# VectorE's order in a fused retention and feed-forward kernel: the product with h ahead of the product of d and r

## The chip, the cores and the metric

The kernel runs on one core of a Trainium2 chip. The metric is the device time of one execution in microseconds (us). Times of the trace are counted from the span's start; a single instruction's duration is given in us or ns.

## What is computed

Three layers follow one another: a retention (an attention with a decay in place of a softmax), a feed-forward layer whose activation is h times tanh(softplus(h)), and a layer of eight experts to which tokens are assigned greedily by their logits. The change lies in the feed-forward layer.

```python
def _moe_ref(x, w_in, w_out):
    h = x @ w_in                       # 2304 x 512 times 512 x 2048
    sp = np.where(h > 20.0, h, np.log1p(np.exp(np.minimum(h, 20.0))))
    g = h * np.tanh(sp)
    return (g @ w_out)
# around it: x = retention(q, k, v); out[mask_e] = relu(x[mask_e] @ w1[e]) @ w2[e]
```

## The kernel before

The first part of the kernel interleaves the retention, the conversion of the feed-forward weights and the feed-forward itself. The 2304 tokens are nine blocks of 256, the 2048 hidden units sixteen slices of 128; `plan()` lists the 144 steps (block n, slice f). One loop runs over the steps i, and every engine works through its instructions in the order in which this loop issues them (the order is written out by hand).

A step has these pieces, with what each engine does in them:

- `ff_h` (L317): twelve TensorE matmuls make h for 128 hidden units and 256 tokens in PSUM (`ph`). Weights and activations are split into a high and a low part, so there are three products for each of four slices of the inner dimension. Two steps share a PSUM bank, and there are two such banks; a bank is written again when both its steps have been read.
- `ff_a1`: ScalarE's tanh, square and scaling (L326 to L328) make two tables d for positive and negative halves; VectorE multiplies them (L334).
- `ff_a2` (L339): VectorE's reciprocal of that product, in place. The result is r.
- `ff_b1` (L344, or L346 and L347): u is the product of d, its halves swapped, and r. As long as weights are being converted (`alone`) this is one instruction of 128x256 on VectorE, and r is a buffer of its own; later it is two instructions of 128x128 on GpSimd. In the last step it is two on VectorE.
- `ff_b2` (L352): VectorE's product of (u - 1) with h, read from PSUM. It is issued for step i-1 in step i. Only then is `ph` of that step free.
- `ff_b3` (L358, L359): ScalarE rounds the result to its high part gh, and VectorE (during conversion) or GpSimd subtracts it to get the low part gl. It is issued for step i-2 in step i.
- `ff_y` (L411, in the last block L447): six (or twelve) TensorE matmuls add to the output, three steps later.

The conversion of one weight slice takes a step too: a load of 512 KB into one of two `raw` buffers, on SP's queue (L140); `x1` and `c` on ScalarE (L159, L156); `x` and `a` on VectorE (L163, L168, both reading two operands from SBUF); `h` on ScalarE (L174), the rounding to a high part; and `l` on GpSimd (L177), the subtraction that leaves the low part. `a` is the last reader of its raw buffer, and the next load is issued behind it. In the order of the loop, `x` and `a` of the current slice come first, then the step's own pieces with `x1` of the next slice between `ff_a1` and `ff_b3`, then `h` and `c`.

In a step with conversion VectorE's order is thus L163, L168, L334, L359, L339, L344, L352, and ScalarE's is L326, L327, L328, L159, L358, L174, L156. In the steps up to about 84 us pieces of the retention come in between (GpSimd's share of them is L228 and L233), and some steps behind that have no conversion.

Of the kernel before, what the change touches and what calls it, by code (L numbers as in the profile page):

```python
# [64 lines left out]
def plan():  # L65


    spread = lambda a, b, n: [a + (b - a) * k // (n - 1) for k in range(n)]
    own = {i: (0, f) for f, i in enumerate([0, 1, 2, 3] + spread(6, ENDS[0], NF - 4))}
    free = [i for i in range(3 * NF) if i not in own]  # L70
    lead = [i for i in free if i < BEGIN2]
    rest = [i for i in free if BEGIN2 <= i]
    near = [i for i in rest if i <= ENDS[1]]
    ones = lead + [near[k] for k in spread(1, len(near) - 1, NF - len(lead))]
    own.update({i: (1, f) for f, i in enumerate(ones)})
    own.update({i: (2, f) for f, i in enumerate(i for i in free if i not in ones)})
    steps = [own[i] for i in range(3 * NF)]
    steps += [(n, f) for n in range(3, NB) for f in range(NF)]
    return steps


def first_part(ctx, tc, att, att_ht, att_hn, dtab, qtab, ktab, stab, wi, wo, wgb, ydram, L, constants, cst, begin, grid):
    nc = tc.nc
# [15 lines left out]
    steps = plan()  # L99
# [42 lines left out]
    class convert:  # L142
# [18 lines left out]
        def x(self):  # L161
            w0 = self.w0
            nc.vector.scalar_tensor_tensor(w0, self.w1, 0x80000000, w0, op0=ALU.bitwise_and,  # L163
                                           op1=ALU.bitwise_or)
# [144 lines left out]
    def ff_h(n, f, i):  # L309
        xh, xl = x_block(n)  # L310
        if i % 2 == 0:
            hbank[0] = psum.tile([P, 2, TB], F32, tag=("ph0", "ph1")[i // 2 % 2], name="ph")
        ph = hbank[0][:, i % 2, :]
        k = 0
        for kt in range(KT):
            for w, x in ((winh, xh), (winl, xh), (winh, xl)):
                nc.tensor.matmul(ph, w[f][:, kt, :], x[:, kt, :], start=(k == 0), stop=(k == 11))  # L317
                k += 1
        q2[n, f] = ph

    def ff_a1(n, f, i, alone):

        ph = q2[n, f]
        d = work.tile([P, 2, P], F32, tag="d", name="d", bufs=2)
        df = d.rearrange("p a b -> p (a b)")
        nc.scalar.activation(df, ph, AF.Tanh, scale=0.5)  # L326
        nc.scalar.activation(df, df, AF.Square, bias=half_b, scale=-0.5)  # L327
        nc.scalar.activation(df, df, AF.Copy, bias=0.5, scale=0.5)  # L328
        u = work.tile([P, 2, P], F32, tag="u", name="u", bufs=3)
        r = u[:, 0, :]  # L330
        if alone:

            r = work.tile([P, DM], BF, tag="scr", name="r").bitcast(F32)[:, :P]
        nc.vector.tensor_mul(r, d[:, 0, :], d[:, 1, :])  # L334
        inv[n, f] = (d, u, r, alone)

    def ff_a2(n, f):
        r = inv[n, f][2]
        nc.vector.reciprocal(r, r)  # L339

    def ff_b1(n, f, eng):
        d, u, r, alone = inv.pop((n, f))
        if alone:
            eng.tensor_mul(u, d[:, ::-1, :], r[:, None, :].to_broadcast([P, 2, P]))  # L344
        else:
            eng.tensor_mul(u[:, 1, :], d[:, 0, :], r)  # L346
            eng.tensor_mul(u[:, 0, :], d[:, 1, :], r)  # L347
        gt[n, f] = u.rearrange("p a b -> p (a b)")

    def ff_b2(n, f):  # L350
        g = gt[n, f]
        nc.vector.scalar_tensor_tensor(g, g, -1.0, q2.pop((n, f)), op0=ALU.add, op1=ALU.mult)  # L352

    def ff_b3(n, f, eng):
        g = gt[n, f]
        gh = work.tile([P, TB], F32R, tag="gh", name="gh", bufs=3)
        gl = work.tile([P, TB], F32R, tag="gl", name="gl", bufs=3)
        nc.scalar.activation(gh, g, AF.Copy)  # L358
        eng.tensor_sub(gl, g, gh.bitcast(F32))  # L359
        gt[n, f] = (gh, gl)  # L360
# [170 lines left out]
    for i in range(len(steps) + YL):  # L531
        new = i < len(steps)
        if i == 20:
            constants()
        if i == 62:
            stage.__exit__(None, None, None)
            late = tc.tile_pool(name="late", bufs=1)
            WG = late.__enter__().tile([P, E, DM], F32, name="WG")
            nc.sync.dma_start(WG, wgb)
        if now:  # L540
            now.x()
            now.a()
        if old:
            old.l()
        if new:
            n, f = steps[i]
            ff_h(n, f, i)
            for x in slots.get(i, []):
                x()
            ff_a1(n, f, i, bool(now or old))  # L550
        if nxt and i in CONV:
            nxt.x1()
        if new:

            eng = nc.vector if now or old else nc.gpsimd
            if i > 1:
                ff_b3(*steps[i - 2], eng)
            ff_a2(n, f)
            ff_b1(n, f, nc.vector if i == len(steps) - 1 else eng)
            if i:  # L560
                ff_b2(*steps[i - 1])
        if i == len(steps) - 1:
            ff_b2(n, f)
            ff_b3(*steps[i - 1], nc.gpsimd)
            ff_b3(n, f, nc.vector)
        if now:
            now.h()
        old, now = now, None
        if nxt and i in CONV:
            now, nxt = nxt, convert() if done[0] < len(parts) else None  # L570
            now.c()
        for k in range(2 if i % 4 == 0 or TAIL <= i < POP2 else 1):
            if idle:
                idle.pop(0)()
        if late and i > TAIL + BEGIN and not idle:
            late = late.__exit__(None, None, None)
            soon.extend(begin())
        if i >= YL:
            ff_y(*steps[i - YL], i)
# [840 lines left out]
def build(tc, ap, out):  # L1420
    nc = tc.nc
    with ExitStack() as ctx:
        pp = ctx.enter_context(tc.tile_pool(name="pp", bufs=1))
        dp = ctx.enter_context(tc.tile_pool(name="dp", bufs=1, space=bass.MemoryType.DRAM))
        cp = ctx.enter_context(tc.tile_pool(name="cp", bufs=1))
        ctx.enter_context(tc.manual_schedule())
        L = pp.tile([P, NT, E], F32, name="L")
        ydram = dp.tile([N, DM], F32, name="ydram")
        cst = {}
        start = []  # L1430
        cs = ExitStack()

        def begin():
            start.append(Search(cs, tc, L, cst))
            return start[0].early()

        with ExitStack() as c1:
            first_part(c1, tc, ap["att"], ap["att_ht"], ap["att_hn"], ap["dtab"], ap["qtab"],
                       ap["ktab"], ap["stab"], ap["wi"], ap["wo"], ap["wgb"], ydram, L, lambda: constants(cp, tc, ap, cst), cst, begin, lambda *a: Grid(cs, tc, L, cst).pieces(*a))
        keep = ctx.enter_context(tc.tile_pool(name="keep", bufs=1, reuse_waits="tile"))  # L1440
        L0 = keep.tile([P, NT, E], F32, name="L0")
        nc.gpsimd.tensor_copy(L0, L)
        with ExitStack() as c2:
            flag = second_part(c2, tc, L, ydram, ap["wx"], cst, out, start[0], True, L0)
            again = nc.values_load(flag[0:1, 0:1], min_val=0, max_val=1)
        cs.close()
        with tc.If(again != 0):
            with ExitStack() as c3:
                general_constants(c3, tc, ap, cst)
                second_part(c3, tc, L0, ydram, ap["wx"], cst, out, Start(c3, tc, L0, cst), False)  # L1450
# [15 lines left out]
def constants(cp, tc, ap, cst):  # L1466
    nc = tc.nc
    load_constants(cp, tc, ap, cst, (("ident", [P, P], F32), ("J", [P, NJ + 1], F32), ("SCL", [P, 3], F32),
                                     ("pri", [P, E], F32), ("tri", [P, P], BF), ("io", [P, 96], BF),
                                     ("pcv", [P, NT, 2], BF), ("WGN", [P, KT, E], F32)))  # L1470
    cst["ones"] = cp.tile([P, P], BF, name="c_ones")
    nc.vector.memset(cst["ones"], 1.0)
# [69 lines left out]
```

## Time and profile before

| | us |
|---|---|
| median of 3 runs | 856.23 |
| lowest and highest of them | 855.38, 856.98 |
| the profiled execution | 856.09 |
| its span, first to last instruction | 854.2 |

| engine | busy us | share of the span |
|---|---|---|
| TensorE matmuls | 781.2 | 91% |
| VectorE | 556.4 | 65% |
| GpSimd | 476.0 | 56% |
| ScalarE | 438.5 | 51% |

The shares are averages over unlike stages. The steps with weight conversion run from 31 to 171 us of the span, the other feed-forward steps up to about 551 us, the expert layer from there to the end. A line of the timeline has an instruction's start, its duration, engine, source line and operands; in square brackets stands how long its engine had stood idle before it, and what ended that. An instruction's recorded end can lie a little behind the start of the next one on the same engine.

### The profile page before, as it was taken

How to read it: one execution, taken by the hardware profiler on the slowest of the kernel's cores; microseconds unless marked ns; L12 is line 12 of the kernel's file. 1: busy time of each engine (PE TensorE's matmuls, PEld its weight loads, DVE VectorE, ACT ScalarE, POOL GpSimd, SP SyncE). 2: the span in 40 equal slices, each digit the busy share in tenths (PEclk: the TensorE clock that was granted, in tenths of full speed). 3: DMA queues.
4: the chain of work that ended last, by engine and by line, in shares of the span. 5: the costliest groups of instructions: out<-in, count | busy, mean ns of one | idle time of the engine just before them, and what ended most of it. 6: DMA issues, size and time to landing. Idle time of an engine off the chain costs nothing.

```text
span 854.2 us, 16245 instructions
## 1 busy us (share of the span) xinstructions
PE 781.2 (91%) x6151; PEld 711.9 (83%) x6151; DVE 556.4 (65%) x1271; ACT 438.5 (51%) x963; POOL 476.0 (56%) x541
## 2 busy tenths in 40 slices
PE   6787778799999999999999999939999999999993
PEld 5676566698899888889888989838999899999993
DVE  4797999964654689788897885576566643532210
ACT  2676777754554445454455464423344543654521
POOL 2533332354554666667666664413777986977911
PEclk9798999999999999999999999957999999999997
DMA  8535332201024120111210000033665656555411
GB/s 310 179 117 181 140 130 101 74 26 48 30 73 148 52 74 25 51 52 49 76 50 26 1 26 2 2 133 127 200 184 175 186 174 185 163 159 185 127 30 31
DMA packets 27320, 87.63 MB, mean 103 GB/s; under 512 B 4448, under 2 KB 5600, under 8 KB 27104
## 3 DMA queue, kind: packets, MB, share of 16 engines
q1 hardware_dynamic: 24160, 77.06, 27.8%
q0 software_dynamic: 3072, 9.44, 3.4%
q8 instruction: 50, 0.82, 0.4%
q14 instruction: 38, 0.31, 0.1%
HBM read 77.05 MB, written 9.44 MB: 101 GB/s over the span
## 4 chain that ended last, share of the span: by engine, by line
PE 70%; DVE 12%; issue 6%; ACT 4%; DMA 4%; POOL 2%; SPq 0%; DVEq 0%; POOLq 0%; ACTq 0%
PE ph L317 20%; PE hp L1257 9%; PE op L1271 8%; PE b_E L411 8%; PE b_F L411 7%; PE cnt L972 2%; DVE r L339 2%; DMA raw<-in_wi_dram 2%; DVE u L344 1%; PE b_A L219 1%; DVE raw L163 1%; PE b_D L248 1%; DVE hot L868 1%; PE b_E L447 1%; PE b_F L447 1%
## 5 line engine op out<-in xcount | busy, mean ns | idle before, releaser
L317 PE MATMUL ph<-xh,winh 128*128 128x256 f32 x576 | 165.6, 287 | 16.8 <-DVE u L352 9.7
L317 PE MATMUL ph<-xl,winh 128*128 128x256 f32 x576 | 163.1, 283 | 0.2 <-DVE xl L255 0.2
L317 PE MATMUL ph<-xh,winl 128*128 128x256 f32 x576 | 163.2, 283 | 0.0
L811 POOL TENSOR_TENSOR wxl<-wraw,wxh 128x1024 fp32r<-128x1024 f32 x60 | 142.4, 2397 | 31.3 <-ACT wxh L809 30.8
L359 POOL TENSOR_TENSOR gl<-u,gh 128x256 fp32r<-128x256 f32 x114 | 86.0, 754 | 90.1 <-ACT gh L358 89.4
L317 PEld LDWEIGHTS ph<-xh,winh 128*128 128x128 f32 x576 | 110.5, 192 | 29.0 <-DVE u L352 15.1
L326 ACT ACTIVATE d<-ph 128x256 f32<-128x256 f32 x144 | 54.9, 381 | 135.7 <-PE ph L317 122.0
L317 PEld LDWEIGHTS ph<-xh,winl 128*128 128x128 f32 x576 | 111.3, 193 | 4.5
L317 PEld LDWEIGHTS ph<-xl,winh 128*128 128x128 f32 x576 | 111.5, 194 | 0.4 <-DVE xl L255 0.4
L339 DVE RECIPROCAL u<-u 128x128 f32<-128x128 f32 x113 | 107.7, 953 | 3.9
L334 DVE TENSOR_TENSOR u<-d 128x128 f32<-128x128 f32 x113 | 45.4, 402 | 63.6 <-ACT d L328 55.8
L346 POOL TENSOR_TENSOR u<-d,u 128x128 f32<-128x128 f32 x112 | 52.5, 469 | 52.5 <-DVE u L339 52.3
L809 ACT ACTIVATE wxh<-wraw 128x1024 fp32r<-128x1024 f32 x64 | 67.3, 1052 | 17.9 <-DMA wraw<-in_wx_dram 17.9
L327 ACT ACTIVATE d<-d,half_b 128x256 f32<-128x256 f32 x144 | 73.5, 510 | 4.7
L347 POOL TENSOR_TENSOR u<-d,u 128x128 f32<-128x128 f32 x112 | 68.4, 610 | 8.8
L328 ACT ACTIVATE d<-d 128x256 f32<-128x256 f32 x144 | 60.2, 418 | 4.6
L358 ACT ACTIVATE gh<-u 128x256 fp32r<-128x256 f32 x144 | 58.0, 403 | 4.1 <-DVE u L352 4.1
L368 DVE SCALAR_TENSOR_TENSOR scr<-y,WG 128x512 bf16<-128x512 f32 x64 | 55.3, 864 | 0.4
L1248 DVE SCALAR_TENSOR_TENSOR htl<-hp,hth 128x288 fp32r<-128x288 f32 x64 | 28.4, 454 | 40.4 <-ACT hth L1260 38.8
L352 DVE SCALAR_TENSOR_TENSOR u<-u,ph 128x256 f32<-128x256 f32 x144 | 53.9, 375 | 0.2
L1260 ACT ACTIVATE hth<-hp 128x288 fp32r<-128x288 f32 x64 | 26.2, 409 | 52.9 <-PE hp L1257 46.7
L177 POOL TENSOR_TENSOR wol<-y,woh 128x512 fp32r<-128x512 f32 x16 | 20.7, 1292 | 54.5 <-ACT woh L174 54.5
(271 smaller groups left out, 1942.3 us busy)
## 6 DMA issues: line engine op xcount, KB each, us to landing
wraw<-in_wx_dram SPq DMA_DIRECT2D x64, 512.0 KB, 4.5
att<-in_att_dram SPq DMA_DIRECT2D x32, 512.0 KB, 5.2
raw<-in_wi_dram SPq DMA_DIRECT2D x16, 512.0 KB, 3.5
raw<-in_wo_dram SPq DMA_DIRECT2D x16, 512.0 KB, 3.3
ydram<-y SPq DMA_DIRECT2D x9, 512.0 KB, 2.8
WG<-in_wgb_dram SPq DMA_DIRECT2D x1, 2048.0 KB, 7.7
att<-in_att_ht_dram SPq DMA_DIRECT2D x4, 256.0 KB, 4.1
att<-in_att_hn_dram SPq DMA_DIRECT2D x4, 256.0 KB, 4.7
```

The costliest lines, as they stand in the source:

```text
L317: nc.tensor.matmul(ph, w[f][:, kt, :], x[:, kt, :], start=(k == 0), stop=(k == 11))
L327: nc.scalar.activation(df, df, AF.Square, bias=half_b, scale=-0.5)
L328: nc.scalar.activation(df, df, AF.Copy, bias=0.5, scale=0.5)
L339: nc.vector.reciprocal(r, r)
L347: eng.tensor_mul(u[:, 0, :], d[:, 1, :], r)
L358: nc.scalar.activation(gh, g, AF.Copy)
L359: eng.tensor_sub(gl, g, gh.bitcast(F32))
L411: nc.tensor.matmul(py[n][t], g[:, t * P:(t + 1) * P], w[f], start=(f == 0 and w is woh and g is gh), stop=(f == NF - 1 and g is gl))
L809: nc.scalar.activation(hi, raw, AF.Copy)
L811: rest = lambda eng: eng.tensor_sub(lo, raw, hi.bitcast(F32))
L1257: nc.tensor.matmul(hp, W[kt][w][:, s], x[:, kt, :], start=(k == 0), stop=(k == 11))
L1271: nc.tensor.matmul(op, W[4 + ft // 2][w][:, s], h[:, ft, :], start=(k == 0), stop=(k == 23))
```

## The change

`ff_b2` of the step before is issued ahead of `ff_b1` of the current step. It was issued behind it.

```diff
--- before.py
+++ after.py
@@ -556,9 +556,9 @@
             if i > 1:
                 ff_b3(*steps[i - 2], eng)
             ff_a2(n, f)
-            ff_b1(n, f, nc.vector if i == len(steps) - 1 else eng)
             if i:
                 ff_b2(*steps[i - 1])
+            ff_b1(n, f, nc.vector if i == len(steps) - 1 else eng)
         if i == len(steps) - 1:
             ff_b2(n, f)
             ff_b3(*steps[i - 1], nc.gpsimd)
```

Where `ff_b1` runs on VectorE (the 31 steps with a conversion under way, and the last step), VectorE's order changes from L339, L344, L352 to L339, L352, L344. Where it runs on GpSimd, the two pieces stand on different engines.

## Rows read from the trace of the kernel before

**Rows 1.** Stretches: start:end, length, busy us (x instructions) of each engine, clock, DMA.

```profile
84.00:132.00 48.00, 36.40 (x204) 28.41 (x203) 45.11 (x82) 37.65 (x81) 15.51 (x12) 1.00 0.41 140
132.00:171.00 39.00, 32.47 (x181) 26.53 (x182) 36.33 (x69) 29.56 (x65) 10.37 (x8) 0.96 0.24 82
190.00:300.00 110.00, 110.00 (x841) 98.82 (x841) 60.86 (x114) 54.51 (x136) 57.69 (x96) 1.00 0.21 71
```

**Rows 2.** Waits of TensorE from 171 to 560 us: total us, times, longest.

```profile
PE ph L317 <- DVE u L352: 0.4, 1, 0.4
```

**Rows 3.** Timeline of one pass, VectorE, ScalarE, GpSimd and SP's queue.

```profile
95.11 0.69 DVE L168 SCALAR_TENSOR_TENSOR y<-y,raw 128x512 uint32<-128x512 uint32 x1
...
95.83 0.33 SPq L140 DMA_DIRECT2D raw<-in_wi_dram  x1
...
96.26 0.95 DVE L339 RECIPROCAL r<-r 128x128 f32<-128x128 f32 x1
...
96.55 1.30 POOL L177 TENSOR_TENSOR winl<-y,winh 128x512 fp32r<-128x512 f32 x1 [2.75 <-ACT winh L174]
...
97.24 0.88 DVE L344 TENSOR_TENSOR u<-d,r 128x256 f32<-128x256 f32 x1
...
98.05 0.41 DVE L352 SCALAR_TENSOR_TENSOR u<-u,ph 128x256 f32<-128x256 f32 x1
98.38 0.68 DVE L163 SCALAR_TENSOR_TENSOR raw<-raw 128x512 uint32<-128x512 uint32 x1
...
99.12 0.69 ACT L159 ACTIVATE raw<-raw 128x512 uint32<-128x512 uint16 x1 [0.84 <-DMA raw<-in_wi_dram]
99.16 0.69 DVE L168 SCALAR_TENSOR_TENSOR y<-y,raw 128x512 uint32<-128x512 uint32 x1
...
100.15 0.42 DVE L359 TENSOR_TENSOR gl<-u,gh 128x256 fp32r<-128x256 f32 x1
...
100.49 0.94 DVE L339 RECIPROCAL r<-r 128x128 f32<-128x128 f32 x1
```

**Rows 4.** The weight loads issued from 84 to 171 us.

```profile
DMA to landing us min/median/max: 3.1/3.3/4.0
```

**Rows 5.** L344 from 84 to 171 us, L352 from 28: ns min/median/max.

```profile
L344 DVE TENSOR_TENSOR u<-d,r x22: 426/848/886, 85.0 to 170.0; 128x256 f32<-128x256 f32 x22
...
L352 DVE SCALAR_TENSOR_TENSOR u<-u,ph x30: 404/408/415, 37.8 to 170.3; 128x256 f32<-128x256 f32 x30
```

**Rows 6.** Timeline of VectorE, the first step whose L346 is on GpSimd.

```profile
170.98 0.95 DVE L339 RECIPROCAL u<-u 128x128 f32<-128x128 f32 x1
171.85 0.36 DVE L352 SCALAR_TENSOR_TENSOR u<-u,ph 128x256 f32<-128x256 f32 x1
```

**Rows 7.** Timeline around the break in the conversions, VectorE and TensorE.

```profile
129.98 0.95 DVE L339 RECIPROCAL r<-r 128x128 f32<-128x128 f32 x1
...
131.75 0.41 DVE L352 SCALAR_TENSOR_TENSOR u<-u,ph 128x256 f32<-128x256 f32 x1
...
132.21 0.38 PE L317 MATMUL ph<-xh,winh 128*128 128x256 f32 x1 [1.36 <-DVE u L352]
```

**Rows 8.** Timeline at the end of the conversions, VectorE and TensorE.

```profile
163.72 0.41 DVE L352 SCALAR_TENSOR_TENSOR u<-u,ph 128x256 f32<-128x256 f32 x1
...
164.18 0.39 PE L317 MATMUL ph<-xh,winh 128*128 128x256 f32 x1 [0.93 <-DVE u L352]
...
170.80 0.39 PE L317 MATMUL ph<-xh,winh 128*128 128x256 f32 x1 [0.44 <-DVE u L352]
```

**Rows 9.** Waits of TensorE from 47 to 84 us for VectorE.

```profile
PE b_B L411 <- DVE xl L255: 2.7, 1, 2.7
```

**Rows 10.** The chain that ended last, in the last feed-forward step.

```profile
548.87 0.30 DVE u L346
...
551.13 0.74 PE b_E L447 x4
```

**Rows 11.** A stretch behind the break, columns as in rows 1.

```profile
132.00:136.00 4.00, 3.79 (x16) 3.50 (x17) 3.58 (x8) 2.12 (x6) 0.00 (x0) 0.58 0.02 6
```

## The prediction, made before the changed kernel ran

> **What bounds the kernel now.** I read the stretches first [rows 1]. From 190 to 300 us TensorE is busy in every microsecond, and between 171 and 560 us it waits for L352 once, for 0.4 us [rows 2], so whatever the stage before gains is handed on whole. In that stage (84 to 171 us, one feed-forward step with one weight conversion in nearly every pass) VectorE is the full engine: 45.11 of 48.00 us, against 36.40 on TensorE. So I next read the order of events in one pass [rows 3].
>
> Call R the start of a step's reciprocal (L339) and A the end of L168, which frees a raw buffer for the next weight load. On VectorE alone: A = 95.11 + 0.69 = 95.80, R = 96.26 (0.46 later, with L334 and L359 between), the next A = 99.16 + 0.69 = 99.85 (3.59 after R). That is 4.05 us a step. A second loop is just as long: the A at 95.80 issues a load at 95.83, ScalarE's L159 takes it at 99.12 (3.29 us), L358 follows it in ScalarE's order, L359 of VectorE waits for L358 until 100.15, and the reciprocal comes at 100.49. From A to the R two steps on this is 4.69 us; with 3.59 from R to A it makes 8.28 us for two steps, 4.14 each. ScalarE had stood idle for 0.84 us until the load came, and the loads of this stage land in 3.1 to 4.0 us [rows 4]. So the stage has two limits close together, and both hold the stretch from R to A.
>
> **What is odd in that stretch.** L344, the step's product of d and r, starts at R + 0.98 and its follower comes 0.81 us later, at 98.05 [rows 3]. Of the 22 between 84 and 171 us the shortest took 426 ns, the median 848 ns [rows 5]. Beside the long ones GpSimd runs its weight subtraction L177 (96.55 to 97.85). L344 reads two operands from SBUF; with a follower about 0.34 us behind its true start when free (0.43 less the 0.08 by which the next one starts ahead of a recorded end), it truly started at 98.05 - 0.34 = 97.71, that is R + 1.45, just as L177 ended. So VectorE stands still for 0.47 us in a pass. L352, the product with h, reads h from PSUM: all 30 of them took 404 to 415 ns [rows 5], with GpSimd at work or not, so it doesn't wait for GpSimd.
>
> **The change part by part.** No instruction is added or removed, none of it issues a DMA, and SP's and ScalarE's orders stay. On VectorE L352 of the step before goes ahead of L344.
>
> - *L352 earlier.* Behind a reciprocal that it doesn't need, L352 starts after 171.85 - 170.98 = 0.87 us [rows 6]; L344, which needs it, after 0.98 [rows 3]. So L352 moves from R + 1.79 (98.05 - 96.26) to R + 0.87. Its cost of 0.33 us (98.05 to 98.38) now lies in VectorE's wait.
> - *L344 later.* It can start at 0.87 + 0.33 = R + 1.20, still before GpSimd's end at R + 1.45; it waits 0.25 and ends where it did. What is queued behind it (L163, L168) starts at R + 1.45 + 0.34 = R + 1.79 in place of R + 2.12 (98.38). R to A falls from 3.59 to 3.26 us. Its result is read by L352 only in the next step. The buffer r is next written by L334, behind it on its own engine; d has two buffers, and the tanh that overwrites this one stands behind ScalarE's L159 of 99.12, a microsecond after L344's end at 98.12. Neither costs anything.
> - *What this is worth.* VectorE alone would need 0.46 + 3.26 = 3.72 us a step. The loop through the load needs 4.69 + 3.26 = 7.95 for two, 3.97 each for this load of 3.29 us. It binds, so the gain is 0.33 us for two steps, not for one: what is late next is the load, seen as L359 waiting for L358. With no load in the way it would be 0.33 a step; if loads grew longer as they come closer, nothing. I take the half, as the load's row is the one that is nearest to the limit.
>
> The sum over the stage, followed from the first blocked L344 at 85.0 us:
> 1. Eleven steps up to R = 129.98: 5.5 loops of 0.33 = 1.8 us.
> 2. The break behind that [rows 7]: a step without conversion, in which TensorE's ph matmuls stood 1.36 us until L352 (131.75) had freed their bank, and then ScalarE's tanh, L358 and L359 waited for them. There L352 itself sets the time, and it moves from R + 1.77 to R + 0.87: 0.9 us.
> 3. Six steps behind the break: 3 loops of 0.33 = 1.0 us.
> 4. The last stretch [rows 8]: TensorE's run from 164.18 starts behind the L352 of 163.72, which I take to lie as far behind its R as at the break: 0.9 us again. The pause of 0.44 ahead of 170.80 closes too, as that L352 comes earlier still: 0.4 us. From there TensorE doesn't pause.
>
> Together 1.8 + 0.9 + 1.0 + 0.9 + 0.4 = 5.0 us.
>
> At the two places where TensorE waits for L352 its new start counts. By a sentence of the Trainium skill (VectorE: DVE Perf Modes, The DRAIN you can't avoid) the next VectorE operation doesn't start until the pipe is empty, whether or not a semaphore is waited on. L352 would then start at R + 0.98, as L344 did, those two places would give 0.8 each, and the stage 4.8. The trace speaks against it here: 0.87 and 0.98 stand in [rows 6] and [rows 3].
>
> - *The first nine passes (31 to 84 us).* From 47 us on TensorE waits for VectorE there only once, right at the start [rows 9]; behind that the chain runs over TensorE and ScalarE. For three passes ahead of it (31 to 47 us), each handing on its 0.33 to that wait, 1.0 us would be won; if L163, now 0.33 earlier, got ahead of GpSimd's products of the retention and these came late, as much could be lost. Between ends so close, and with VectorE and GpSimd in each other's way there in either order, I take 0.
> - *Steps with the product on GpSimd (171 to 548 us).* Each engine keeps its order; only the last step has both on VectorE. I take 0; a loss only if GpSimd waited for L352 too, 0.36 a step [rows 6], and it would first have to use up what keeps TensorE without a pause there [rows 1, 2].
> - *The last step [rows 10].* There the two products of 0.30 us (L346, and L347 like it) stand ahead of L352 in the chain to GpSimd's L359 and TensorE at 551.13. L352 moves ahead of both: 0.6 us. The last step's own L352 stays where it was.
>
> Sum: 5.0 + 0 + 0.6 = 5.6 us. The profiled execution took 856.09 us (span 854.2 and 1.9 around it), 0.14 below the median of 856.23. 856.09 - 5.6 = 850.5 us.
>
> **The rivals.**
> - *The load doesn't bind.* If loads land at the short end (3.1 us) and ScalarE's order slips less than I think, VectorE alone sets the step: 0.33 in each of 17 steps, 5.6 in place of the 2.8 of points 1 and 3, so 847.7. For it: the loop is only 0.1 longer than VectorE's own now. Against: L359 already waits for L358 at 100.15.
> - *The loads stretch.* Closer together, they take 3.6 in place of 3.3 us; the loop gives back its 0.33, and points 2 and 4 with the tail remain: 2.2 + 0.6 = 2.8, so 853.3. For it: one took 4.0. Against: at 3.97 us a step they still don't overlap.
> - *The wait stays.* If L344 is long for another reason than L177 (by its place behind the reciprocal, say) or L352 now takes the wait, the pass keeps its length; the change doesn't do what it says. Only the tail's 0.6 remains: 855.5. Against: L352's 404 to 415 ns.
> - *Slower: the clock falls more often.* Behind the pause of 1.36 us at 132.21 TensorE's granted clock was 0.58 in the next four microseconds [rows 11], so at the lower of its two levels (1.2 GHz) for most of them; that costs about (1 - 0.58) x 4 = 1.7 us of its work. The change shifts all pauses of this kind (0.93 and 0.44 in [rows 8]). It decides from the fourth further fall on that lies where TensorE is late: 850.5 + 4 x 1.7 = 857.3, beyond 0.2% above the median at the fifth (859.0). Against: the pauses get shorter with the step.
>
> **How the numbers follow.** The forecast (850.5) has 0.62; the load that doesn't bind 0.13; loads that stretch 0.12; the wait that stays 0.09; the clock 0.04. The forecast's own range is 849.0 to 852.0, its terms being uncertain by the 1.0 of the first passes and half a microsecond of the places where L352 sets the time. Eight in ten are reached with most of the two neighbours: 847.4 to 853.4. A measurement of this kernel can tell about 0.2% (1.7 us) from no change. Faster by more than that are the first three cases, 0.87; within it the wait that stays and part of the clock, 0.09; slower 0.04.
>
> **What would show it.** In the profile after, between 80 and 166 us: L352 directly behind L339, 0.87 us on, and still at most 0.42 us long; L344's median near 0.43 + 0.25 - 0.08 = 0.60 us in place of 0.85; two steps in 7.8 to 8.0 us; L359's idle time for L358 up, since it now absorbs what VectorE saves; TensorE's last pause at 165.8 in place of 170.80, and its reading of the last gl near 545.5 in place of 551.13. If L344 stays at 0.85, the cause of its length was wrong; if the steps fall to 3.7 us, the load didn't bind; if L159 still waits as long in steps of 4.1 us, the loads stretched.

## The result: 848.0 us in place of 856.6, and the profile after

| | before | after |
|---|---|---|
| median, same chip | 856.61 | 847.98 |
| lowest and highest | 855.38, 857.07 | 847.39, 849.51 |
| the profiled execution | 856.09 | 849.51 |
| its span | 854.2 | 847.6 |

The ratio is 0.9904 (95% interval 0.9887 to 0.9921), so the change takes away 8.2 us (6.8 to 9.7). The forecast was a gain of 5.6 us to 850.5, with a range of 847.4 to 853.4. The sign and the place were right, and of the mechanism the main part; the size was too small, and the measured time lies below the 849.0 to 852.0 that the forecast gave its own sum.

The stretches of the kernel after, first; they answer to [rows 1] (start:end, length, then busy us and instructions of TensorE, its weight loads, VectorE, ScalarE and GpSimd, the granted clock, the DMA share and GB/s):

```profile
84.00:132.00 48.00, 39.03 (x219) 31.91 (x218) 42.81 (x86) 38.45 (x84) 14.90 (x12) 0.96 0.40 137
132.00:171.00 39.00, 34.00 (x202) 27.80 (x201) 34.40 (x68) 30.24 (x68) 13.67 (x14) 1.00 0.24 82
190.00:300.00 110.00, 110.00 (x856) 99.08 (x855) 62.85 (x119) 55.33 (x139) 56.50 (x96) 1.00 0.21 73
```

In the first 48 us VectorE gets through 86 instructions in 42.81 busy us, where it had done 82 in 45.11: more work in less busy time. From 190 us on TensorE is still busy without a gap, so what the stage gains is handed on.

One pass of the kernel after, VectorE with SP's queue, GpSimd's L177 and the ScalarE instructions that the load goes through (start, duration, engine, line; in brackets the idle time before it and what ended it). It answers to [rows 3]:

```profile
93.53 0.69 DVE L168 SCALAR_TENSOR_TENSOR y<-y,raw 128x512 uint32<-128x512 uint32 x1
94.25 0.33 SPq L140 DMA_DIRECT2D raw<-in_wi_dram  x1
...
94.68 0.94 DVE L339 RECIPROCAL r<-r 128x128 f32<-128x128 f32 x1
94.96 1.29 POOL L177 TENSOR_TENSOR winl<-y,winh 128x512 fp32r<-128x512 f32 x1 [2.42 <-ACT winh L174]
95.55 0.36 DVE L352 SCALAR_TENSOR_TENSOR u<-u,ph 128x256 f32<-128x256 f32 x1
95.82 0.71 DVE L344 TENSOR_TENSOR u<-d,r 128x256 f32<-128x256 f32 x1
96.46 0.68 DVE L163 SCALAR_TENSOR_TENSOR raw<-raw 128x512 uint32<-128x512 uint32 x1
97.24 0.69 DVE L168 SCALAR_TENSOR_TENSOR y<-y,raw 128x512 uint32<-128x512 uint32 x1
97.41 0.68 ACT L159 ACTIVATE raw<-raw 128x512 uint32<-128x512 uint16 x1 [0.69 <-DMA raw<-in_wi_dram]
97.98 0.41 ACT L358 ACTIVATE gh<-u 128x256 fp32r<-128x256 f32 x1
98.43 0.42 DVE L359 TENSOR_TENSOR gl<-u,gh 128x256 fp32r<-128x256 f32 x1 [0.29 <-ACT gh L358]
98.77 0.94 DVE L339 RECIPROCAL r<-r 128x128 f32<-128x128 f32 x1
```

With R = 94.68, L352 starts at R + 0.87 and takes 0.36 us beside GpSimd's L177; L344 starts 0.27 later and still ends behind L177; L163 starts at R + 1.78 (2.12 before) and L168 ends at R + 3.25 (3.59 before). From R to A 0.34 us are gone, and then the load's turn comes: L159 waited 0.69 us for it, L358 stands behind L159, L359 waited 0.29 us for L358, and the step is 98.77 - 94.68 = 4.09 us long.

The same two groups as in [rows 5], after (ns min/median/max; first and last start). L344's median was forecast at 0.60 us:

```profile
L344 DVE TENSOR_TENSOR u<-d,r x22: 413/664/728, 84.3 to 165.0; 128x256 f32<-128x256 f32 x22
...
L352 DVE SCALAR_TENSOR_TENSOR u<-u,ph x32: 352/361/366, 37.3 to 169.5; 128x256 f32<-128x256 f32 x32
```

L359 from 80 to 171 us, in the kernel before and then after (busy us, mean ns | idle us ahead of it and what ended it): VectorE's wait for gh has grown, as it had to if the load is late next.

```profile
L359 DVE TENSOR_TENSOR gl<-u,gh 128x256 fp32r<-128x256 f32 x22 | 9.3, 422 | 2.9 <-ACT gh L358 2.5
```

```profile
L359 DVE TENSOR_TENSOR gl<-u,gh 128x256 fp32r<-128x256 f32 x22 | 9.3, 424 | 5.1 <-ACT gh L358 4.9
```

TensorE's wait for L352 (line waited for, total us, times, longest), before from 87 to 172 us and after from 84 to 165 us:

```profile
PE ph L317 <- DVE u L352: 9.7, 10, 1.4
PE b_A L411 <- ACT gh L358: 3.9, 5, 1.1
PE b_E L411 <- ACT gh L358: 2.9, 3, 1.2
PE b_C L411 <- ACT gh L358: 1.0, 1, 1.0
```

```profile
PE b_A L411 <- ACT gh L358: 5.5, 7, 2.2
PE b_C L411 <- ACT gh L358: 4.3, 5, 0.9
PE b_E L411 <- ACT gh L358: 3.0, 4, 0.9
PE ph L317 <- DVE u L352: 1.0, 3, 0.4
```

TensorE hardly waits for L352 any more (1.0 us in place of 9.7). Its waits for gh, which comes through ScalarE behind L159, grew from 7.8 to 12.8 us: of the 8.7 us saved at L352 5.0 are waited there. The two pauses of [rows 8] are gone; TensorE's last pause ahead of 172 us ends at 157.34, where 165.8 had been forecast.

The last feed-forward step, after; it answers to [rows 10]:

```profile
542.16 0.95 DVE L339 RECIPROCAL u<-u 128x128 f32<-128x128 f32 x1
...
543.03 0.36 DVE L352 SCALAR_TENSOR_TENSOR u<-u,ph 128x256 f32<-128x256 f32 x1
...
543.92 0.73 POOL L359 TENSOR_TENSOR gl<-u,gh 128x256 fp32r<-128x256 f32 x1 [1.08 <-ACT gh L358]
...
544.71 0.39 PE L447 MATMUL b_E<-gl,woh 128*128 128x256 f32 x1 [0.17 <-POOL gl L359]
```

TensorE reads that gl at 544.71 in place of 551.13, 6.4 us earlier. So nearly all of the 6.6 us between the two profiled executions lies ahead of this point.

### The profile page after: what moved, and what is told of

It reads as the page before. It is cut to its first block, busy times and chain, and to the rows that moved or that the text cites. A ratio compares the mean times of both kernels' runs of the same rounds, so it can differ in the third digit from the quotient of the medians.

```text
span 847.6 us, 16248 instructions
## 1 busy us (share of the span) xinstructions
PE 776.6 (92%) x6151; PEld 709.3 (84%) x6151; DVE 548.1 (65%) x1271; ACT 437.3 (52%) x963; POOL 475.1 (56%) x541
## 4 chain that ended last, share of the span: by engine, by line
PE 72%; DVE 9%; issue 6%; DMA 5%; ACT 4%; POOL 2%; SPq 0%; DVEq 0%; POOLq 0%; ACTq 0%
PE ph L317 20%; PE hp L1257 10%; PE op L1271 8%; PE b_E L411 8%; PE b_F L411 7%; DMA raw<-in_wi_dram 2%; PE cnt L972 2%; PE b_A L219 1%; DVE r L339 1%; PE b_D L248 1%; DVE raw L163 1%; DVE hot L868 1%; POOL wxl L811 1%; DMA raw<-in_wo_dram 1%; PE b_E L447 1%
## 5 line engine op out<-in xcount | busy, mean ns | idle before, releaser
L359 POOL TENSOR_TENSOR gl<-u,gh 128x256 fp32r<-128x256 f32 x114 | 85.8, 753 | 88.3 <-ACT gh L358 87.6
L339 DVE RECIPROCAL u<-u 128x128 f32<-128x128 f32 x113 | 107.7, 953 | 3.9
L334 DVE TENSOR_TENSOR u<-d 128x128 f32<-128x128 f32 x113 | 45.4, 402 | 63.3 <-ACT d L328 55.5
L346 POOL TENSOR_TENSOR u<-d,u 128x128 f32<-128x128 f32 x112 | 52.3, 467 | 52.9 <-DVE u L339 52.8
L358 ACT ACTIVATE gh<-u 128x256 fp32r<-128x256 f32 x144 | 57.9, 402 | 2.1 <-DVE u L352 2.0
L352 DVE SCALAR_TENSOR_TENSOR u<-u,ph 128x256 f32<-128x256 f32 x144 | 52.5, 365 | 0.3
L177 POOL TENSOR_TENSOR wol<-y,woh 128x512 fp32r<-128x512 f32 x16 | 20.6, 1288 | 53.5 <-ACT woh L174 53.5
```

## The experiments

"Gain" below means one minus the ratio, times the time of the kernel before on the same chip (854.3 us in the first group, 856.7 in the second, 854.8 in the third). Step times are differences between starts of the reciprocal.

### Which steps bring the gain

The change as it is, on another chip:

```diff
             ff_a2(n, f)
-            ff_b1(n, f, nc.vector if i == len(steps) - 1 else eng)
             if i:
                 ff_b2(*steps[i - 1])
+            ff_b1(n, f, nc.vector if i == len(steps) - 1 else eng)
```

> The changed kernel as it is, a second profile and more executions. Theory 1 (the trace's 6.6 us of span is the change's own worth, the rest of the difference of medians is TensorE's clock, which rose about 0.9 us later at 28 us in the changed kernel's first profile): executions spread over about 2 us, median 848 to 849.5, ratio 0.990 to 0.992; the marks from 84 to 165 us move by 4.7 against before as in the first profile. Theory 2 (the change is worth 8.6 us everywhere): median 848, span near 845.5 and the marks 84 to 165 us a further 2 us earlier.

Measured: 846.24 us, ratio 0.9907 (0.9893 to 0.9921), a gain of 7.9 us. The ratio is the one that theory 1 named; the time is lower than either theory had it, as the kernel before is 2.3 us faster on this chip too, and so it doesn't tell the two apart.

The new order in the last step alone:

```diff
             ff_a2(n, f)
+            swap = i == len(steps) - 1
+            if i and swap:
+                ff_b2(*steps[i - 1])
             ff_b1(n, f, nc.vector if i == len(steps) - 1 else eng)
-            if i:
+            if i and not swap:
                 ff_b2(*steps[i - 1])
```

> The order of before, with the product with h ahead only in the last of the 144 steps. Theory 1 (my sum): the chain from the tanh of the last step to TensorE's last gl falls by 0.6 to 0.7 us, time 856.0. Theory 2 (the excess of the measured gain over 5.6 sits behind the feed-forward part, where an earlier end shifts the expert part's clock or transfers): 854 to 855.

Measured: 853.63 us, ratio 0.9995 (0.9984 to 1.0006). In the trace the last reciprocal and TensorE's first matmul of the stage behind the feed-forward lie 5.33 us apart; in the kernel before it is 6.08, in the kernel after 5.34. The term is there, 0.7 us, though the timing alone can't tell it from nothing.

The new order in the first nine steps alone (the same diff with another condition):

```diff
+            swap = i < 9
```

> The order of before, with the product with h ahead only in the first nine steps (up to 84 us). Theory 1: 856.6, within 1.0 either way. Theory 2 (these steps hold the excess of about 3 us that my sum lacks): 853.6.

Measured: 854.07 us, ratio 0.9999 (0.9988 to 1.0009): nothing. The passes up to 84 us bring no net gain and no loss.

The new order from the tenth step on, without the last:

```diff
+            swap = 9 <= i < len(steps) - 1
```

> The order of before up to 84 us and in the last step, the new order in all steps between. Theory 1: minus 4.7 to 5.0 us, so 851.6 to 852. Theory 2 (the excess sits in these steps): 849. If the three parts are worth their own amounts, the gains of this run, of the last step alone and of the first nine add up to that of the whole change.

Measured: 848.59 us, ratio 0.9930 (0.9914 to 0.9945), a gain of 6.0 us. With 0.4 and 0.1 us of the other two parts that is 6.5, against 7.9 (6.7 to 9.1) for the whole: the parts add up within the intervals, and the stage of the weight conversions carries the gain. The 6.0 (4.7 to 7.3) lies between theory 1, 4.7 to 5.0, and theory 2, 7.6.

### Does the load bind?

The kernel before and the kernel after, both without the weight loads from the eleventh step on (the conversions then work on what the two buffers hold; the output isn't the reference's):

```diff
+            if i >= 10:
+                raws.append(raws[-2])
+                return
```

> Order of before. Leaves out the weight loads from the eleventh on: the conversion takes what lies in the buffer, so these weights are those of other slices; all instructions of the engines stay. Theory 1 (VectorE and the load bind about equally before): the step falls from 4.10 to VectorE's own 4.05 us; with the few long loads of 120 to 126 us gone too, 1 to 2 us less, 855. Theory 2 (the load doesn't matter): no change, 856.6.

> New order, the same loads left out. Theory 1 (the load binds in the new order): the step falls from 3.93 to 3.72 us, VectorE's idle time ahead of L359 is gone; 17 steps of 0.2 and the long loads make 3 to 5 us less than the changed kernel, 843 to 845. Theory 2 (the load doesn't bind, ScalarE or the product's remaining wait does): steps stay near 3.9, time 848.

Measured: the old order without loads 853.45 us, ratio 0.9967 (0.9952 to 0.9982); the new order without loads 843.92, ratio 0.9855 (0.9829 to 0.9881). Starts of the reciprocal in consecutive steps, first in the old order without loads, then in the new one (the edit moves the line from 339 to 342):

```profile
95.58 0.94 DVE L342 RECIPROCAL r<-r 128x128 f32<-128x128 f32 x1
99.61 0.95 DVE L342 RECIPROCAL r<-r 128x128 f32<-128x128 f32 x1
103.65 0.94 DVE L342 RECIPROCAL r<-r 128x128 f32<-128x128 f32 x1
```

```profile
96.44 0.94 DVE L342 RECIPROCAL r<-r 128x128 f32<-128x128 f32 x1
100.16 0.94 DVE L342 RECIPROCAL r<-r 128x128 f32<-128x128 f32 x1
103.87 0.95 DVE L342 RECIPROCAL r<-r 128x128 f32<-128x128 f32 x1
```

The steps are 4.03 and 4.04 us, and 3.72 and 3.71: VectorE's own 4.05 and 3.72 of the prediction. With the loads the kernel after needs more: 4.0 a step in the mean of the eleven up to the break at 130 us. So "the load doesn't bind" is refuted as a mechanism, although its time (847.7) is close to the one measured: taking the loads away is worth 2.8 us in the old order and 4 to 6 in the new one (12.4 in all, against 6.75 to 8.2 with the loads). For the old order 1 to 2 us had been expected; 2.8 (1.5 to 4.1) is somewhat more. The load is what is late next.

### Was GpSimd's subtraction the cause of the long L344?

In both orders L177 is replaced by a fill with zeros. The weights' low parts are left out, and the expert assignment takes the kernel's second, general path, some 400 us longer; only the first part is compared. The fills wait for nothing that the profile shows and are over by 79 us, so nothing of GpSimd's conversion runs beside L344 in the stage.

```diff
-            nc.gpsimd.tensor_sub(self.lo, self.t, self.hi.bitcast(F32))
+            nc.gpsimd.memset(self.lo.bitcast(F32), 0.0)
```

> Order of before. GpSimd's subtraction L177 is replaced by a fill with zero (the low parts of the weights are left out): GpSimd writes the same tile but reads nothing. Theory 1 (L344 waits for GpSimd's subtraction): L344 falls from 0.85 to 0.43 us in every pass, the loads then bind, and the time is that of the changed kernel or a little less, 847 to 851. Theory 2 (L344 is long by its place behind the reciprocal): it stays at 0.85, 856.6. If a fill holds VectorE up just as a subtraction does, L344 stays long for as long as the fill lasts.

> New order, L177 replaced by the same fill. Theory 1: without the wait the order is worth only the two places where TensorE waits for L352 and the last step, and the 0.17 us by which VectorE's row of three is shorter where loads don't bind: 2 to 3 us less than the run with the order of before and the same fill. Theory 2 (the order itself, not the wait, is the gain): 8 us less than that run.

Measured: 1250.66 and 1242.54 us, of which only the first part counts here. L344 in the stage, old order and then new:

```profile
L344 DVE TENSOR_TENSOR u<-d,r x22: 424/426/426, 84.1 to 164.0; 128x256 f32<-128x256 f32 x22
```

```profile
L344 DVE TENSOR_TENSOR u<-d,r x22: 408/412/416, 80.3 to 157.5; 128x256 f32<-128x256 f32 x22
```

Without the subtraction every L344 takes 0.43 us in the old order, in the same place behind the reciprocal. The median of 848 ns in [rows 5] was GpSimd's doing, and "the wait stays" falls. That agrees with the Trainium skill (SBUF — State Buffer, SBUF: two separate sides), by which a VectorE instruction with two SBUF inputs and a GpSimd instruction that reads SBUF exclude each other for the whole instruction; L352, with one input in PSUM, isn't concerned, and its 352 to 366 ns beside L177 agree.

Over the 22 steps of the stage the old order takes 81.80 us without the subtraction, where it takes 87.2 with it; the new order with the subtraction takes 82.0 (both are means of four of the eight traces that the part on the prediction uses). So taking the wait away is worth as much as the change, which is what theory 1 said of the old order.

But the order is worth something with no wait to fill, too: 79.05 us in place of 81.80, 2.75 us against 5.2 with the subtraction. About half of the stage's gain doesn't need the wait. In the eleven steps up to the break it is 1.2 us (43.65 to 42.49), where the table below has 2.4.

The whole difference of the pair is larger than theory 1 had it: 8.1 us in the times, and 7.9 at TensorE's first matmul behind the feed-forward (548.10 and 540.20). That is the number of theory 2. Of it 0.8 lie ahead of the first reciprocal, where the order plays no part, 3.2 in the first nine steps, 2.75 in the 22 steps and 1.2 behind them. With the subtraction the first nine steps gave nothing; two of them hold 2.1 of the 3.2 here, and what binds those two isn't shown. There is one trace of each kernel.

### Taking VectorE's L359 out of the load's way

L358 is put ahead of L159 in ScalarE's order, so that gh no longer waits behind the load, in the new and in the old order:

```diff
-        if nxt and i in CONV:
-            nxt.x1()
         if new:
...
                 ff_b3(*steps[i - 2], eng)
+        if nxt and i in CONV:
+            nxt.x1()
+        if new:
             ff_a2(n, f)
```

> New order, and on ScalarE the rounding L358 ahead of L159, which waits for the load; nothing is left out. Theory 1 (the load binds because L359 stands behind L358 and L358 behind L159): L359 no longer waits; the load only reaches the step through L159, L174 and L177, 0.57 us behind L159's start, so with a load of 3.29 us the step is 3.72 plus about 0.06, 3.78 in place of 3.93; 17 steps of 0.15 make 2.5 us less than the changed kernel, ratio to before 0.987. Theory 2 (the later L174 and L177 lengthen L344's wait by as much as L359's wait falls): steps stay at 3.9, ratio 0.990.

> Order of before on VectorE, L358 ahead of L159 on ScalarE. Theory 1: VectorE's own 4.05 us binds, the step falls from 4.13 only to 4.05; 17 steps make 1 to 1.5 us, ratio 0.998. Theory 2 (ScalarE's order alone is what matters): 4 us or more, 0.995.

Measured: new order 845.44 us, ratio 0.9887 (0.9869 to 0.9905); old order 852.56, ratio 0.9979 (0.9967 to 0.9991), as theory 1 had it. In the new order L359 doesn't wait any more from 80 to 171 us. Two steps with GpSimd's L177 and VectorE's L344:

```profile
L359 DVE TENSOR_TENSOR gl<-u,gh 128x256 fp32r<-128x256 f32 x22 | 9.2, 419 | 0.0
```

```profile
93.86 0.95 DVE L339 RECIPROCAL r<-r 128x128 f32<-128x128 f32 x1
...
94.53 1.28 POOL L177 TENSOR_TENSOR winl<-y,winh 128x512 fp32r<-128x512 f32 x1 [2.81 <-ACT winh L174]
...
95.00 1.09 DVE L344 TENSOR_TENSOR u<-d,r 128x256 f32<-128x256 f32 x1
...
97.94 0.95 DVE L339 RECIPROCAL r<-r 128x128 f32<-128x128 f32 x1
...
98.22 1.28 POOL L177 TENSOR_TENSOR wol<-y,woh 128x512 fp32r<-128x512 f32 x1 [2.42 <-ACT woh L174]
...
99.08 0.71 DVE L344 TENSOR_TENSOR u<-d,r 128x256 f32<-128x256 f32 x1
...
101.64 0.95 DVE L339 RECIPROCAL r<-r 128x128 f32<-128x128 f32 x1
```

The second step takes 3.70 us, VectorE's own time. The first takes 4.08: L177 ends there 1.95 us behind the reciprocal, in the second 1.56, and L344 is 1.09 us long in place of 0.71. L177 waits for ScalarE's L174, which stands behind L159 and so behind the load. So both theories are right in part, and the ratio lies between their 0.987 and 0.990: the load no longer reaches the step through L359, but in some steps it does through L174, L177 and L344's wait. The eleven steps up to the break take 42.77 us, against 44.08 in the changed kernel and 41.18 without loads; 1.3 of the 2.9 us that the loads cost there come back. The median is 9.4 us below the kernel before in this group and 2.2 us below the changed kernel measured beside it; the second is not clear of noise, as the two intervals overlap at their ends.

### How far can two executions of one kernel lie apart?

The kernel before and the changed kernel once more, unedited, beside the two above:

> The kernel before against itself, for a second profile. Ratio 1.000 within 0.1%. If the fall of TensorE's clock at 132 us belongs to its first profile and not to the kernel, the break from the reciprocal at 130 to that of the second step on takes 6.6 us here as it did in the runs with the last step alone and the first nine alone, not 7.4; if it belongs to the kernel, 7.4.

> The changed kernel once more, on the chip of these four. Theory 1 (5.3 us in the stage, 0.7 in the last step, nothing in the first nine): ratio 0.992 to 0.993. Theory 2 (another 2 us that no stretch of the trace shows): 0.990.

Measured: the kernel before 854.70 us (852.41 to 856.79), ratio 0.9999 (0.9987 to 1.0012); the changed kernel 847.59 (847.19 to 848.23), ratio 0.9921 (0.9904 to 0.9937), a gain of 6.75 us. So the three measurements of the change (8.2, 7.9, 6.75) agree within their intervals, and one trace may lie 2 us from its neighbours. The break from the reciprocal at 130 us took 7.33 us in this second trace of the kernel before, so by the sentence above its slow break would belong to the kernel. But the last step alone and the first nine alone have the old order there too and took 6.59 each: neither reading fits all four, and what decides it is not shown.

## Why the prediction was right, and where its sizes were off

Durations between marks of eight traces, as means of four each. Old order in the stage: before, the last step alone, the first nine alone, before again. New: after, the whole change twice, the one from the tenth step on. (In the row of the last step those with the new order there stand against those without.) The forecast's terms stand beside them:

| part | old, us | new, us | gain | forecast |
|---|---|---|---|---|
| eleven steps up to the break | 46.52 | 44.08 | 2.4 | 1.8 |
| the break, two steps | 6.99 | 6.38 | 0.6 | 0.9 |
| six steps behind it | 24.66 | 23.55 | 1.1 | 1.0 |
| the end of the conversions | 15.16 | 13.79 | 1.4 | 1.3 |
| the last step | 6.06 | 5.34 | 0.7 | 0.6 |

The sum is 6.2 us, against 5.6 forecast. Behind the feed-forward the four traces with the new order in the stage are 0.7 us shorter in the mean (299.18 to 298.44), which would bring 6.9, inside all three intervals; but single traces scatter there by 1.5 us in the old order and 2.6 in the new, so the 0.7 is not shown to be the change's, and the rest up to 7.9 and 8.2 us lies in no stretch that was found.

That the measured 848.0 lies in the range is in part luck. It is below the 849.0 to 852.0 of the forecast's own sum, in the part of the range that stood for the rival "the load doesn't bind" (847.7), and that rival's mechanism holds only in the ninth and the eleventh of the eleven steps. Terms 2 and 4 did not come about as reasoned, as told below.

- *L352 fills the wait.* Right where the wait is: it starts 0.87 us behind the reciprocal, as [rows 6] had it, stays short beside L177, and VectorE alone went from 4.04 to 3.71 us a step. The sentence of the Trainium skill on the empty pipe (VectorE: DVE Perf Modes, The DRAIN you can't avoid) would have had it at 0.98 like L344; the trace after has 0.87 in the pass shown and in the last step. The same section adds that a next operation that isn't held starts earlier; no run here tests what holds one. What the forecast did not see is that about half of the stage's gain would be there without the wait (2.75 of 5.2 us).
- *The load binds, and the gain is halved.* Right in kind: with the loads away the eleven steps fall by another 2.9 us (44.08 to 41.18), with L358 ahead of L159 by 1.3. The size, term 1, was too small by 0.6. In the first eight of the eleven steps two take 8.19 us in the old order and 7.82 in the new (means without before again): 0.37 in place of 0.33, and 7.8 where 7.95 stood. The rest isn't spread over all steps. The ninth step is 4.34 to 4.41 us long in all four old traces and 4.00 to 4.01 in the four new, 0.37 by itself, where I had counted half of 0.33. L168 stands idle there for 0.46 us in either order, with the loads and without, and L359 doesn't wait, so VectorE's own row binds and the gain comes whole. What L168 waits for is open; with L358 ahead of L159 the pause is gone. The eleventh, 4.07 us before and 3.73 after, gives the whole 0.34 too. And before again holds one more step of 5.44 us (the third), which puts 0.35 on the mean of the old order alone. The tenth step, 4.8 to 5.4 us, is as long in either order; without the loads it takes 4.03 and 3.71.
- *The break.* Here the reasoning was wrong, not only the size. I let L352 set the time, because TensorE stood 1.36 us for it [rows 7]. In the profiled execution of before TensorE's granted clock then fell to 0.58 [rows 11]. That it need not fall with this order, and can, the stretch from 132 to 136 us shows in the last-step-alone kernel (the old order there too) and in the kernel before again:

```profile
132.00:136.00 4.00, 3.75 (x26) 3.51 (x27) 3.58 (x8) 3.05 (x8) 0.00 (x0) 1.00 0.03 10
```

```profile
132.00:136.00 4.00, 3.25 (x15) 3.06 (x16) 3.58 (x9) 2.29 (x5) 0.08 (x1) 0.67 0.17 70
```

At 1.00 (2.4 GHz) the break takes 6.59 us, at 0.58 and 0.67 it takes 7.44 and 7.33. The reciprocals of the break at the full clock, old order (last step alone) and new (the whole change):

```profile
130.02 0.94 DVE L339 RECIPROCAL r<-r 128x128 f32<-128x128 f32 x1
...
133.02 0.94 DVE L339 RECIPROCAL r<-r 128x128 f32<-128x128 f32 x1
...
136.61 0.94 DVE L339 RECIPROCAL r<-r 128x128 f32<-128x128 f32 x1
```

```profile
126.38 0.95 DVE L339 RECIPROCAL r<-r 128x128 f32<-128x128 f32 x1
...
129.10 0.95 DVE L339 RECIPROCAL r<-r 128x128 f32<-128x128 f32 x1
...
132.51 0.94 DVE L339 RECIPROCAL r<-r 128x128 f32<-128x128 f32 x1
```

From 3.00 + 3.59 to 2.72 + 3.41 us: 0.46 at the same clock. TensorE's ph run does begin 0.95 us earlier behind R (its pause there is 0.41 us in place of 1.36), but in the second step VectorE works without a gap for 3.59 or 3.41 us and is the bound itself. So the 0.95 was worth at most the 0.28 of the first step, where L359 had waited 0.28 us for gh; the 0.18 of the second are VectorE's own. Where the clock fell in or just ahead of the break, it takes 7.44 and 7.33 us in the old order and 6.63 twice in the new, 0.7 to 0.8 less: the row's 0.6 is a mean over both cases.
- *The last stretch and the last step.* In size right: 1.4 and 0.7. But term 4 repeats the reasoning of the break. From the reciprocal at 161.94 to that at 170.98 VectorE has only one pause before, and it isn't the 0.93 that TensorE stood:

```profile
168.66 0.43 DVE L359 TENSOR_TENSOR gl<-u,gh 128x256 fp32r<-128x256 f32 x1 [0.28 <-ACT gh L358]
```

These three steps take 9.04 us before and 7.96 after (157.66 to 165.62): 0.28 is this pause, the other 0.8 is VectorE's own row. Only the 0.3 of the step behind, where L334 waits for ScalarE's d 1.47 us in place of 1.76, comes from a TensorE that starts earlier. That 0.9 + 0.4 met the 1.4 is luck. In the tail L352 moved not only by the two products of 0.30 but also by the 0.11 us between 0.98 and 0.87.
- *The first nine passes, and the steps with the product on GpSimd.* Right at nothing: 0.9999 for the first, and from the first reciprocal to that at 84 us the traces with the old order there take 51.8 to 53.8 us, those with the new 52.2 to 52.8. From the end of the conversions to the last reciprocal the old traces have 370.70 to 370.97 us, the new 370.67 to 370.96.
- *The rivals.* "The load doesn't bind", "the wait stays" and "the loads stretch" fall: the loads landed in 3.2 to 4.5 us with the same median of 3.3 as in [rows 4]. "The clock falls more often" falls too: a lower clock in the break or just ahead of it came in two of the four traces with the old order in the stage (before, before again) and in two of the four with the new one.
- *Not forecast: the stage behind.* The first long group of matmuls of the expert layer, in the chain that ended last, before and then after:

```profile
581.08 5.26 PE hp L1257 x20
```

```profile
574.98 4.38 PE hp L1257 x20
```

The granted clock in the stretch that begins some 33 us behind TensorE's reading of the last gl (551.13 and 544.71), before and then after:

```profile
584.00:588.00 4.00, 4.00 (x34) 3.54 (x33) 0.96 (x5) 0.50 (x2) 0.00 (x0) 0.67 0.16 64
```

```profile
578.00:582.00 4.00, 4.00 (x42) 3.65 (x41) 1.79 (x7) 1.61 (x3) 0.00 (x0) 0.98 0.07 29
```

TensorE comes from a pause at 0.50 (1.2 GHz) and is back at 2.4 GHz sooner after. In the three traces of the change and that of the change from the tenth step on this group took 4.2 to 4.5 us, in those of the old order 4.8 to 5.3. But with L358 ahead of L159 it took 5.1 in the new order as well. Why the clock comes back sooner is open, and so whether the change causes it; in the pair of profiled executions the whole stage behind differs by only 0.2 us.

## What to carry to other kernels

Where an instruction stands still because another engine works on the same memory (here both read SBUF), look behind it in its queue for one that isn't held up by that engine (here one that reads h from PSUM) and needs nothing of the waiting one, and let it go first. Then ask what the new order is worth with the wait gone: here it was about half. Before counting the gain once per step, close the second loop, here load, ScalarE, VectorE: about half of the gain of a plain step stayed there, and a second reordering, of two ScalarE instructions, brought part of it back in the trace. And a stall of one engine is worth its length only if no other engine works through the same stretch without a gap; one trace may also hold a clock that the next execution doesn't.

## What the runs showed of the hardware that was not expected

- The order is worth something on VectorE without any contention. Behind the reciprocal L352 starts after 0.87 us and L344 0.28 after it, where L344 had started after 0.98 and L352 0.34 after it (the runs without the subtraction). In the second step of the break, which has no subtraction beside L344, this is the 3.41 in place of 3.59 us.
- L352, with 404 to 415 ns on record behind L344, has 352 to 366 ns behind the reciprocal: the recorded duration of one and the same operation depends on what stands ahead of it.
- Executions of the kernel before alone lie between 852.4 and 858.2 us over all chips, and TensorE's granted clock in the break with the old order is 0.58, 0.67 or 1.00.
